# Side work of a gated-MLP kernel's feed-forward and output stages: places from formulas, places from tables

## The chip, the cores and the metric

The kernel runs on one core of one Trainium2 chip. Its time is the device time of one launch in microseconds; a figure is the median of several runs. A core has five engines that each work through a list of their own in order: TensorE (PE in the profile, its weight loads PEld), VectorE (DVE), ScalarE (ACT), GpSimd (POOL) and SyncE (SP). SP only issues DMA transfers here. The engines wait for each other through semaphores.

## The reference

The input x has 2048 tokens of 640 features. With xn = layernorm(x), the kernel computes x + s * silu(B). B is a feed-forward layer, s a linear attention with 32 heads of 20 features and a learned feature map.

```python
B = gelu(xn @ w1 + b1) @ w2 + b2                 # 640 -> 1536 -> 640
q, k, v = heads(xn @ wqkv)
pq, pk = q @ w_phi, k @ w_phi                    # per head, 20 x 20
phi_q = concat(softmax(pq), softmax(-pq))        # 40 features
phi_k = concat(softmax(pk), softmax(-pk))
kv, z = phi_k.T @ v, sum(phi_k)
s = ((phi_q @ kv) / (phi_q @ z + 1e-6)) @ wo
out = x + s * silu(B)
```

## The kernel before

Products of 32-bit numbers are made from three faster products: each operand is split into a high part (one ACT copy that rounds) and a low part (a subtraction on DVE or POOL), and high x high, high x low and low x high are added in PSUM. The large products also use Strassen's scheme with seven block products, which is why sums and differences of blocks (T2, T3, T1, T4 of the activations, S1 to S4 of the weights) are made beside the products.

A first stage, not touched here, projects q, k and v, accumulates kv, and writes the exponentials of the 16 query tiles (128 tokens each, 640 KB) to memory, `e_dram`. The stage after it has an order written out by hand, under `tc.manual_schedule()`, so every engine's list is the order of the program text. It consists of 188 slots:

- slots 0 to 41 (UP0 = 0), first up pass: `up(g)` for the six groups g of hidden features, seven slots each, one block product (`part`) a slot; the results go through gelu into the tiles `hr`;
- slots 42 to 83 (DN0), first down pass, `down(2, ...)`: seven runs of six slots, one for each block product with w2 (A11, A12, S2, S3, S1, S4, A22 in this order), then silu, and the result goes to `g_dram`;
- slots 84 to 125 (UP1) and 126 to 167 (DN1): the same for the other half of the tokens;
- from slot 168 (OUT): the output, four chunks c of 512 tokens with five slots d each: `finish` multiplies the numerators oT with wo, and DVE and POOL multiply with the gate and add x.

A slot first issues its products and what takes them out of PSUM, and then `tick()` runs the side work that is due: functions put into the table `todo` by `when(slot, function)`. Side work is issued at the end of its slot, in the order in which it was entered; `soon(1, ...)` puts work at the head of the next slot, `after(k, ...)` k slots later. An engine executes its list as soon as its waits allow, so a slot is a place in five lists and not a time. The side work is:

- **query tiles** (`plan_q`): `q_load` (SP, from `e_dram`), `q_ez` (POOL, L1536: times the sums of the keys), `q_rc` (DVE, L405 and L1540), `q_dn` (DVE, L1545 to L1552, into a PSUM bank), `q_scale` (POOL, L410), `q_store` (SP, to `phi_dram`). Before, a tile that starts at slot s has them at s-4, s, s+1, s+3, s+4 and s+7;
- **weights of the down products**: `w_load` and `w_make` load and split blocks of w2 (tiles `w2r`, `w2s`); `w_sum` and `w_a35` load the finished sums S1 to S4 that `plan_s` made in slots 2 to 51 (`s_load`, `s_sums`, `s_split`, `s_a35`) and stored to `s_dram`. Before, a block is loaded six slots ahead of its first product, a w2 block split four slots ahead;
- **weights of the second up pass**: in the first up pass `w1_sums`, `w1_step` and `w1_put` make and store them, in the second `w1_raw`, `w1_sum_tiles`, `w1_wa` and `w1_wb` load them and split what is left;
- **forms** (`form`): six slots ahead of a down product, the activation block is split: ACT makes the high part (L1313); for the low part, "bank" has ACT copy the block into a PSUM bank as well (L1312) and DVE subtracts from the bank, "vector" and "pool" subtract straight from SBUF on DVE or POOL (L1317). Before, the first six forms of a pass alternate "pool" and "vector", the other 36 are "bank";
- **reload** and **plan_x**: the operands of the second up pass;
- **numerators**: `load_phi_tile` loads query features, `num_t` transposes them on PE (L1575), `num_m` multiplies with kv (L1586, L1593) and issues small transfers oT<-oTl from ACT's queue. For chunk 0 they lie in the second down pass, for the others in the chunk before.

All loads and stores but oT<-oTl are issued by SP, in one list. `q_store` of a tile and a `store` of a result wait there for the engine that makes it.

## Time and profile before

| | |
|---|---|
| median of 3 runs | 662.82 us (662.77 to 664.23) |
| the profiled execution | 664.42 us |
| its span, first to last instruction | 662.4 us, TensorE clock 1.000 |
| DMA | 154.63 MB, mean 233 GB/s |
| read and written in memory | 98.31 MB, 53.54 MB |

A profile shows one execution. Every instruction has the line of the program that issued it and the names of the tiles that it writes and reads; busy times are sums over instructions, and an idle time is named by what ended it. A product of 128x512 is shown with some 390 ns although the next one starts 230 ns after it, because products overlap in the array. TensorE's idle time is therefore read from the gaps between products, and not from the durations.

### The profile page before, as it was taken

How to read it: one execution, taken by the hardware profiler on the slowest of the kernel's cores; microseconds unless marked ns; L12 is line 12 of the kernel's file. 1: busy time of each engine (PE TensorE's matmuls, PEld its weight loads, DVE VectorE, ACT ScalarE, POOL GpSimd, SP SyncE). 2: the span in 40 equal slices, each digit the busy share in tenths (PEclk: the TensorE clock that was granted, in tenths of full speed). 3: DMA queues.
4: the chain of work that ended last, by engine and by line, in shares of the span. 5: the costliest groups of instructions: out<-in, count | busy, mean ns of one | idle time of the engine just before them, and what ended most of it. 6: DMA issues, size and time to landing. Idle time of an engine off the chain costs nothing. (4 is left out here: it accounts for less than half of the span.)

```text
span 662.4 us, 12226 instructions
## 1 busy us (share of the span) xinstructions
PE 641.4 (97%) x4544; PEld 558.7 (84%) x4544; DVE 453.7 (68%) x718; ACT 387.5 (59%) x693; POOL 439.8 (66%) x382
## 2 busy tenths in 40 slices
PE   9999999999999999999999999998998999999897
PEld 9999999999899998788777888886776787777776
DVE  5878987766875777566896568788998645364142
ACT  4556777644666678556987763223686596513320
POOL 3597887774873467998898756778799620453222
PEclk9999999999999999999999999999999999999999
DMA  8436911032814859885999979773559967989644
GB/s 316 185 120 211 298 62 61 26 97 80 256 81 149 304 206 369 316 299 194 385 319 321 390 268 369 256 276 131 198 206 279 409 227 224 348 294 322 203 147 133
DMA packets 86411, 154.63 MB, mean 233 GB/s; under 512 B 6320, under 2 KB 47792, under 8 KB 85840
## 3 DMA queue, kind: packets, MB, share of 16 engines
q1 hardware_dynamic: 86032, 153.20, 66.0%
q10 hardware_dynamic: 320, 0.66, 0.5%
q8 instruction: 36, 0.59, 0.4%
q14 instruction: 23, 0.19, 0.1%
HBM read 98.31 MB, written 53.54 MB: 229 GB/s over the span
## 5 line engine op out<-in xcount | busy, mean ns | idle before, releaser
L1402 PE MATMUL pB<-hs,w2s 128*128 128x512 f32 x648 | 153.4, 393 | 6.8 <-DMA w2s<-s_dram 1.8
L1402 PEld LDWEIGHTS pB<-hs,w2s 128*128 128x128 f32 x648 | 119.9, 188 | 35.1 <-issue 4.2
L1199 PE MATMUL pB<-xp,w1s 128*128 128x512 f32 x324 | 80.5, 391 | 3.3 <-POOL w1s L1247 1.7
L1199 PE MATMUL pB<-xd,w1s 128*128 128x512 f32 x324 | 79.8, 390 | 0.9 <-POOL w1s L1247 0.9
L1199 PEld LDWEIGHTS pB<-xp,w1s 128*128 128x128 f32 x324 | 60.5, 188 | 17.6 <-DVE pB L1220 2.1
L1648 PE MATMUL pB<-oT,wo 128*128 128x512 f32 (+1 forms) x315 | 71.7, 383 | 2.6 <-DMA oT<-oTl 2.6
L1199 PEld LDWEIGHTS pB<-xd,w1s 128*128 128x128 f32 x324 | 60.7, 188 | 13.9 <-POOL w1s L1247 1.3
L1648 PEld LDWEIGHTS pB<-oT,wo 128*128 128x128 f32 x315 | 56.3, 188 | 15.7 <-issue 2.7
L1254 ACT ACTIVATE hr<-pB,b1t 128x512 f32<-128x512 f32 x48 | 32.6, 686 | 59.1 <-DVE pB L1220 58.8
L1651 POOL TENSOR_TENSOR xres<-gt,xres 128x256 f32<-128x256 f32 x36 | 25.7, 736 | 54.9 <-DVE gt L1650 26.1
L1317 DVE TENSOR_TENSOR hs<-pB,hs 128x512 fp32r<-128x512 f32 x72 | 46.5, 677 | 13.5 <-ACT hs L1313 11.5
L391 POOL TENSOR_TENSOR e<-e,mxs 128x1280 f32<-128x1280 f32 x12 | 28.4, 2371 | 40.4 <-DVE mxs L386 36.0
L1313 ACT ACTIVATE hs<-hr 128x512 fp32r<-128x512 f32 x84 | 52.2, 623 | 2.0 <-PE pB L1402 2.0
L1650 DVE TENSOR_TENSOR gt<-pB,gt 128x256 f32<-128x256 f32 x40 | 15.3, 419 | 54.6 <-PE pB L1648 51.0
L1312 ACT ACTIVATE pB<-hr 128x512 f32<-128x512 f32 x72 | 42.8, 594 | 16.8 <-POOL hr L1299 7.1
L1299 POOL TENSOR_TENSOR hr<-hr 128x512 f32<-128x512 f32 x36 | 49.1, 1388 | 0.0
L397 ACT ACTIVATE e<-e 128x1280 f32<-128x1280 f32 x32 | 40.7, 1273 | 13.5 <-POOL e L391 5.6
L493 PE MATMUL pW<-wsum,xd 128*128 128x320 f32 x288 | 48.4, 310 | 0.0
L410 POOL TENSOR_TENSOR eq<-eq,rc 128x1280 f32<-128x1280 f32 x14 | 33.4, 2385 | 22.0 <-DVE rc L1552 12.1
L493 PEld LDWEIGHTS pW<-wsum,xd 128*128 128x128 f32 x288 | 43.6, 188 | 0.0
L1578 ACT ACTIVATE ph<-pB 120x512 f32<-120x512 f32 (+1 forms) x44 | 23.1, 600 | 33.6 <-PE pB L1575 20.8
L1536 POOL TENSOR_TENSOR ez<-eq,zrep 128x1280 f32<-128x1280 f32 x14 | 42.0, 2998 | 1.1 <-PE pB L1402 1.1
(235 smaller groups left out, 1397.1 us busy)
## 6 DMA issues: line engine op xcount, KB each, us to landing
w2s<-s_dram SPq DMA_DIRECT2D x24, 512.0 KB
e_dram<-e SPq DMA_DIRECT2D x16, 640.0 KB
phi<-phi_dram SPq DMA_DIRECT2D x16, 640.0 KB
eq<-e_dram SPq DMA_DIRECT2D x14, 640.0 KB
phi_dram<-eq SPq DMA_DIRECT2D x14, 640.0 KB
raw<-in_w_dram SPq DMA_DIRECT2D x24, 320.0 KB
w_dram<-w1s SPq DMA_DIRECT2D x12, 512.0 KB
s_dram<-ws SPq DMA_DIRECT2D x12, 512.0 KB
```

The lines of the kernel that those rows point to most:

```text
L397: nc.scalar.activation(ef, ef, AF.Exp)
L410: eng.tensor_tensor(e3, e3, rc[:, :, None].to_broadcast([P, 64, DH]), op=OP.mult)
L493: nc.tensor.matmul(self.bank[ch][:, :HALF], self.x(blk, a), w(b), start=new and i == 0, stop=i == len(mms) - 1, skip_group_check=True)
L1199: nc.tensor.matmul(bank[ch][:], tl[:, a, off + wo_:off + wo_ + P], mov(blk, b), start=new and n == 0, stop=n == len(mms) - 1, skip_group_c ...
L1254: nc.scalar.activation(dst, ps, AF.Gelu_apprx_tanh, bias=b1t[:, f:f + 1])
L1299: nc.gpsimd.tensor_tensor(block(k, g), block(a, g), block(b, g), op=OP.subtract)
L1312: nc.scalar.activation(ps[:], src, AF.Copy)
L1313: nc.scalar.activation(hs[:, 0], src, AF.Copy)
L1317: (nc.gpsimd if lo == "pool" else nc.vector).tensor_tensor(hs[:, 1], ps[:] if lo == "bank" else src, hs[:, 0].bitcast(F32), op=OP.subtract)
L1402: nc.tensor.matmul(ps[:], w(b), hs[:, a, :], start=start and n == 0, stop=stop and n == 2, skip_group_check=True)
L1536: nc.gpsimd.tensor_tensor(qz[t], qe[t], zf[0], op=OP.mult)
L1648: nc.tensor.matmul(ps[:, cols], w, o[:, a, cols], start=n == 0, stop=n == 14)
```

## The change

The formulas that gave the slots of the side work are replaced by a table, `PLAN`, with one number for each piece of work. A number can have a fraction: `when` puts the work into slot `int(s)`, and `tick` sorts a slot's work by the fraction and then by the order of entry; work from `soon` still comes first. The numbers differ from those of the formulas by up to some tens of slots for query tiles (the tiles are also taken in another order: 0, 8, 2, 3, 11, 4, 10, 12, 1, 5, 9, 7, 6, 13, 15, 14) and mostly by less than three slots elsewhere. The low parts of 19 of the 84 forms are made in another way (`lo`). In the output, the phi tiles of a later chunk are loaded at other d (`phi2`). The assertions check that a load from `phi_dram`, `s_dram` or `a35_dram` comes behind its store. No instruction of the products is added or removed.

```diff
@@ -41,6 +41,105 @@
 
 def _ft(t):
     return (120 * t, 120 if t < 10 else 80)
+
+
+PLAN = {
+    "q": [
+        [44, 49, 50, 51, 52, 55],
+        [107.25, 111.25, 114.25, 116.25, 117.25, 120.5],
+        [77, 82, 84, 85.5, 86, 87.5],
+        [79, 83, 87, 89, 102, 107],
+        [89.5, 94, 95, 97, 98, 104.25],
+        [113, 115, 118, 120, 121, 126],
+        [135.25, 139.5, 141.75, 143.0, 147.5, 149],
+        [126.25, 131.25, 131.25, 132.75, 135.25, 138.25],
+        [46.5, 50.5, 51.5, 54.0, 54.5, 57.25],
+        [129, 131, 130.5, 133, 136, 139],
+        [100.75, 102.75, 103.75, 106.75, 108.0, 109.75],
+        [84, 88, 89, 90.5, 92, 93],
+        [105, 109.25, 109, 111, 112, 119],
+        [142.5, 149.5, 147.5, 149.5, 150.5, 154],
+        [168, 170.5, 170, 171, 175, 175.75],
+        [168, 168.75, 169, 170.5, 171, 172],
+    ],
+    "s": [
+        [2.5, 6.0, 8.5, 10.5, 11.5],
+        [7.75, 12.75, 14.75, 18.0, 16.25],
+        [15, 20, 22, 23, 24],
+        [22, 27, 29, 30, 30.5],
+        [26.75, 32, 34.25, 35, 39],
+        [36, 41, 42.5, 43, 44],
+    ],
+    "w": [
+        [36, 38],
+        [40.5, 40.5],
+        [40, 40],
+        [42, 42.25],
+        [44, 44],
+        [44.75, 48],
+        [72, 74],
+        [70, 76],
+        [72, 76],
+        [35, 37],
+        [35.5, 37.5],
+        [40.25, 40.25],
+        [120.5, 123.25],
+        [122, 124],
+        [123.5, 127],
+        [125.5, 127.5],
+        [128, 129.5],
+        [129, 131.5],
+        [156, 158],
+        [158, 159],
+        [160.5, 162],
+        [119.25, 121],
+        [121, 123],
+        [120, 125],
+    ],
+    "ws": [
+        [47.75, 50.75, 51.75, 53.75, 57, 57.5, 66, 68, 70, 59.5, 59.75, 63.75, 60.75, 62.75, 64.75],
+        [132.5, 135.5, 134.5, 137.5, 137.5, 141.5, 149.5, 151.5, 156.0, 143.5, 145.5, 147.5, 144.5, 146.0, 148.5],
+    ],
...
+    "w1_0": [
+        [],
+        [1, 2, 2, 4, 6, 7, 8.25],
+        [7.5, 8.5, 9.5, 10.5, 12.5, 14, 15, 3],
+        [14, 15, 16.25, 17.25, 19, 21, 21, 11],
+        [20, 20, 21, 22, 24, 25, 26, 14],
+        [29, 30, 30.5, 32, 34, 35, 36, 24],
+    ],
+    "phi": [135.75, 135.0, 142.5, 141.5, 166, 163.75, 166.25, 166.25],
+    "num": [152, 152, 154, 156.25, 158.0, 158.5, 156.75, 156, 160, 161.5, 162, 165.25],
...
+    "lo": [
+        ["pool", "vector", "pool", "vector", "pool", "vector", "bank", "bank", "bank", "bank", "vector", "bank", "bank", "bank", "bank", "bank", "bank", "vector", "bank", "vector", "vector", "bank", "bank", "bank", "bank", "bank", "bank", "bank", "bank", "bank", "vector", "bank", "bank", "bank", "bank", "bank", "pool", "pool", "bank", "vector", "bank", "bank"],
+        ["pool", "bank", "pool", "pool", "pool", "vector", "bank", "bank", "bank", "bank", "bank", "bank", "bank", "bank", "bank", "vector", "bank", "bank", "bank", "bank", "bank", "bank", "bank", "bank", "bank", "vector", "bank", "bank", "vector", "pool", "bank", "vector", "bank", "bank", "vector", "bank", "bank", "vector", "pool", "pool", "bank", "bank"],
+    ],
+    "out": [
+        [(6, 0), (5, 0), (0, 11)],
+        [(6, 0), (5, 0), (0, 11)],
+        [(6, 0), (5, 0), (0, 11)],
+    ],
+    "phi2": [
+        [0, 1, 3, 3],
+        [0, 0, 2, 2],
+        [],
+        [],
+    ],
+}
 
 
 @with_exitstack
@@ -1219,20 +1318,20 @@
     def add(out, a, b, eng=nc.vector, op=OP.add):
         eng.tensor_tensor(out, a, b, op=op)
 
-    todo, at_slot = {}, [0]
-
-    def when(s, f, *args):
-        assert s >= at_slot[0]
-        todo.setdefault(s, []).append((f, args))
+    todo, at_slot, seen = {}, [0], set()
+
+    def when(s, f, *args, first=False):
+        assert int(s) >= at_slot[0]
+        todo.setdefault(int(s), []).append((not first, s % 1, len(todo.get(int(s), ())), f, args))
 
     def after(k, f, *args):
         when(at_slot[0] + k, f, *args)
 
     def soon(k, f, *args):
-        todo.setdefault(at_slot[0] + k, []).insert(0, (f, args))
+        when(at_slot[0] + k, f, *args, first=True)
 
     def tick():
-        for f, args in todo.pop(at_slot[0], ()):
+        for *_, f, args in sorted(todo.pop(at_slot[0], ()), key=lambda e: e[:3]):
             f(*args)
         at_slot[0] += 1
 
@@ -1343,26 +1442,22 @@
 
     def w_sum(k, d):
         t = slab(F32R, "w2s", (P, 2, 2, 2 * P))
+        assert {("s", SUMS.index(k) // 2 * 2, g) for g in (2 * d, 2 * d + 1)} <= seen
         load(t[:].bitcast(F32), s_dram[SUMS.index(k)][:, 2 * d:2 * d + 2])
         wt[k, d] = t
 
     def w_a35(d):
+        assert {("a35", 0, g) for g in (2 * d, 2 * d + 1)} <= seen
         load(wt["A5", d][:, :, :, P:].bitcast(F32), a35_dram[:, 2 * d:2 * d + 2])
 
-    def plan_w(s):
-        for i, k in enumerate(("A11", "A12", "S2", "S3", "S1", "S4", "A22")):
+    def plan_w(h):
+        for i, k in enumerate(("A11", "A12", "A22", "A5")):
             for d in range(3):
-                use = s + 6 * i + 2 * d
-                if i == 0:
-                    when(use - 7, w_load, "A5", d)
-                    when(use - 5, w_make, "A5", d, use - 5 > s)
-                if k in SUMS:
-                    when(use - 6, w_sum, k, d)
-                else:
-                    when(use - 6, w_load, k, d)
-                    when(use - 4, w_make, k, d, use - 4 > s)
-        for d in range(3):
-            when(s + 19 + 2 * d, w_a35, d)
+                s, m = PLAN["w"][12 * h + 3 * i + d]
+                when(s, w_load, k, d)
+                when(m, w_make, k, d, m > (DN0, DN1)[h])
+        for i in range(15):
+            when(PLAN["ws"][h][i], w_sum if i < 12 else w_a35, *(((SUMS[i // 3],) if i < 12 else ()) + (i % 3,)))
 
     rws, sts = {}, {}
 
@@ -1382,20 +1477,19 @@
         st = sts[g]
         t = cell((P, 2, 2, 2 * P), F32R, "ws")
         split_late(st[:, k:k + 2], t[:, :, 0, :], t[:, :, 1, :], nc.vector)
+        after(3, seen.add, ("s", k, g))
         store(3, s_dram[k:k + 2, :, g].rearrange("k p b c -> p k b c"), t[:].bitcast(F32))
 
     def s_a35(g):
         src = rws.pop(g)[:, 9]
         t = halves.tile([P, 2, P], F32R, tag="U", name="a35")
         split_late(src, t[:, 0], t[:, 1], nc.vector)
+        after(3, seen.add, ("a35", 0, g))
         store(3, a35_dram[:, g], t[:].bitcast(F32))
 
-    def plan_s(g, s):
-        when(s - 5, s_load, g)
-        when(s, s_sums, g)
-        when(s + 2, s_split, g, 0)
-        when(s + 3, s_a35, g)
-        when(s + 4, s_split, g, 2)
+    def plan_s(g):
+        for s, f, *a in zip(PLAN["s"][g], (s_load, s_sums, s_split, s_a35, s_split), *[(g,) * 5], (None, None, 0, None, 2)):
+            when(s, f, *[b for b in a if b is not None])
 
     def mm3(ps, w, hs, start, stop):
         for n, (a, b) in enumerate(PASSES):
@@ -1411,7 +1505,7 @@
         def step():
             n = at_step[0]
             at_step[0] += 1
-            form(n + AHEAD, los(n + AHEAD))
+            form(n + AHEAD, (los + [None] * AHEAD)[n + AHEAD])
             sum_step()
             tick()
 
@@ -1504,12 +1598,9 @@
         dst = xd()[:, :, :, at(p)]
         split_late(tt[:, a:b], dst[:, a:b, 0, :], dst[:, a:b, 1, :], nc.gpsimd)
 
-    def plan_x(p, s):
-        when(s - 4, xf_load, p)
-        when(s, xf_add, p)
-        when(s + 2, xf_sums, p)
-        when(s + 4, xf_split, p, 0, 4)
-        when(s + 5, xf_split, p, 4, 9)
+    def plan_x(p):
+        for s, f, a in zip(PLAN["x"][p], (xf_load, xf_add, xf_sums, xf_split, xf_split), ((), (), (), (0, 4), (4, 9))):
+            when(s, f, p, *a)
 
     tailp = []
 
@@ -1555,13 +1646,16 @@
         scale_heads(qe[t], qr.pop(t))
 
     def q_store(t):
+        seen.add(t)
         load(phi_dram[t], qe.pop(t))
 
-    def plan_q(t, s, pace=(-4, 0, 1, 3, 4, 7)):
-        for f, k in zip((q_load, q_ez, q_rc, q_dn, q_scale, q_store), pace):
-            when(s + k, f, t)
+    def plan_q(*tiles):
+        for t in tiles:
+            for f, s in zip((q_load, q_ez, q_rc, q_dn, q_scale, q_store), PLAN["q"][t]):
+                when(s, f, t)
 
     def load_phi_tile(c, i, home=None):
+        assert TPC * c + i in seen
         t = (home or slab)(F32R, "phi", (P, 2 * D))
         nc.sync.dma_start(t[:].bitcast(F32), phi_dram[TPC * c + i])
         return t
@@ -1604,6 +1698,7 @@
         for nt, nm in plan:
             now = [(j, p, *num_t(phi, p, j)) for j, p in steps[:nt]]
             del steps[:nt]
+            assert len(turned) >= nm
             for j, p, n, ph in turned[:nm]:
                 num_m(j, oT, p, n, ph)
                 if p and j < 5:
@@ -1682,22 +1777,16 @@
         when(0, q_put, ea[o], 6 + o)
         when((2, 9)[o], q_put, eb[o], 14 + o)
     for g in range(1, NG):
-        s = UP0 + 7 * (g - 1)
-        if g > 1:
-            when(s - 4, w1_next, g)
-        when(s + 1, w1_sums, g)
-        for i, k in enumerate((2, 3, 4, 6)):
-            when(s + k, w1_step, g)
-        for i in range(2):
-            when(s + 7 + i, w1_put, g, i)
+        for s, f, *a in zip(PLAN["w1_0"][g], (w1_sums,) + (w1_step,) * 4 + (w1_put,) * 2 + (w1_next,) * (g > 1), (g,) * 8,
+                            (None,) * 5 + (0, 1, None)):
+            when(s, f, *[b for b in a if b is not None])
     for g in range(NG):
-        plan_s(g, (7, 13, 20, 27, 34, DN0 + 2)[g])
-    LO = lambda n: "bank"
+        plan_s(g)
     for h in range(2):
         s = (DN0, DN1)[h]
         for n in range(AHEAD):
-            when(s - AHEAD + n, form, n, ("pool", "vector")[n % 2])
-        plan_w(s)
+            when(s - AHEAD + n, form, n, PLAN["lo"][h][n])
+        plan_w(h)
     for g in range(NG):
         up(g)
 
@@ -1707,15 +1796,13 @@
         spare.extend(range(4))
 
     when(DN0, start_q)
-    plan_q(0, DN0 + 4)
-    plan_q(1, DN0 + 8)
+    plan_q(*range(16))
     when(DN0 + 16, spare.clear)
     when(DN0 + 17, xds.clear)
-    for i in range(4):
-        when(DN0 + 2 + 4 * i, reload, i)
-        when(DN0 + 18 + 4 * i, reload, 4 + i)
+    for i in range(8):
+        when(PLAN["reload"][i], reload, i)
     for p in range(2):
-        plan_x(p, DN0 + 22 + 7 * p)
+        plan_x(p)
 
     def w1_raw(g):
         w1r_at[g] = load_w1(g, cell)
@@ -1737,24 +1824,17 @@
         w1g_at[g] = w1_dict(w1b.pop(g) + [sl])
 
     for g in range(NG):
-        s = UP1 + 7 * (g - 1)
-        when(s - 3, w1_raw, g)
-        when(s - 1, w1_sum_tiles, g)
-        when(s + 1, w1_wa, g)
-        when(s + 3, w1_wb, g)
+        for s, f in zip(PLAN["w1"][g], (w1_raw, w1_sum_tiles, w1_wa, w1_wb)):
+            when(s, f, g)
     when(UP1 + 9, kv_state, kvr_out[0])
-    for i in range(8):
-        plan_q(2 + i, UP1 - 1 + 5 * i)
-    down(2, LO)
+    down(2, PLAN["lo"][0])
     for g in range(NG):
         up(g)
 
     xstack.close()
     tailp.append(ctx.enter_context(tc.tile_pool(name="late", bufs=8, side="right", reuse_waits="tile")))
     tailp.append(ctx.enter_context(tc.tile_pool(name="phs", bufs=14, side="right", reuse_waits="tile")))
-    for i in range(4):
-        plan_q(10 + i, DN1 + (4, 7, 10, 17)[i])
-    phi, phin, oTs, groups = [], [], {}, {}
+    phi, phin, oTs, groups = {}, {}, {}, {}
 
     def first_oT():
         oTs[0] = new_oT()
@@ -1765,35 +1845,31 @@
         next(groups[0], None)
 
     for i in range(4):
-        when(DN1 + 9 + 3 * i, lambda i=i: phi.append(load_phi_tile(0, i, tall)))
-        when(DN1 + 36 + i, lambda i=i: phin.append(load_phi_tile(1, i)))
+        when(PLAN["phi"][i], lambda i=i: phi.update({i: load_phi_tile(0, i, tall)}))
+        when(PLAN["phi"][4 + i], lambda i=i: phin.update({i: load_phi_tile(1, i)}))
     when(DN1 + 26, first_oT)
-    for n in range(11):
-        when(DN1 + 27 + n, first_num)
-    when(DN1 + 38, first_num)
+    for s in PLAN["num"]:
+        when(s, first_num)
     for j in range(5):
-        when(DN1 + 21 + 2 * j, load_wo)
-        when(DN1 + (26, 28, 30, 32, 38)[j], split_wo)
+        when(PLAN["wo"][j], load_wo)
+        when(PLAN["wo"][5 + j], split_wo)
     for i in range(2):
         when(DN1 + 40 + i, load_res, i)
-    down(0, LO)
+    down(0, PLAN["lo"][1])
 
     oT = oTs[0]
-    for i in range(2):
-        plan_q(14 + i, OUT + 2 + 2 * i, (-2, 0, 0, 1, 2, 3))
     for c in range(NCH):
         nxt, phi2 = iter(()), []
         if c + 1 < NCH:
             oTn = new_oT()
-            nxt = num_groups(phin, oTn, ((6, 0), (5, 0), (0, 11)))
+            nxt = num_groups(phin, oTn, PLAN["out"][c])
         for d in range(KC):
             load_res(c * KC + d + 2)
             finish(c, d, oT, c == NCH - 1 and d >= 3)
             next(nxt, None)
             tick()
-            if c + 2 < NCH and d in (0, 2):
-                for _ in range(2):
-                    phi2.append(load_phi_tile(c + 2, len(phi2)))
+            for _ in range(PLAN["phi2"][c].count(d)):
+                phi2.append(load_phi_tile(c + 2, len(phi2)))
         if c + 1 < NCH:
             oT, phin = oTn, phi2
     while todo:
```

14 lines of the change are left out of this document (added).

## The prediction

> **What bounds the kernel now.** I read the head of the page first: span, then busy time of each engine.
>
> ```profile
> span 662.4 us, 12226 instructions
> PE 641.4 (97%) x4544; PEld 558.7 (84%) x4544; DVE 453.7 (68%) x718; ACT 387.5 (59%) x693; POOL 439.8 (66%) x382
> ```
>
> TensorE is the bound, and the change adds and removes no product. It can only win back time in which TensorE stands still. The busy times by stage say where that is; the columns are the stretch, its length, then busy time and instruction count of PE, PEld, DVE, ACT and POOL, then granted clock, DMA share and GB/s. The stretches are the first up pass, the first down pass, the end of the second up pass, most of the second down pass, the output, and its end.
>
> ```profile
> 239.00:314.00 75.00, 74.12 (x327) 60.89 (x326) 49.03 (x62) 49.49 (x81) 68.53 (x64) 1.00 0.80 288
> 314.00:391.70 77.70, 76.88 (x334) 61.96 (x333) 54.87 (x82) 62.37 (x117) 62.29 (x49) 1.00 0.97 347
> ...
> 430.00:470.00 40.00, 36.73 (x158) 29.05 (x157) 33.99 (x51) 14.24 (x26) 32.25 (x16) 1.00 0.53 188
> 470.00:525.00 55.00, 48.96 (x210) 38.68 (x210) 47.05 (x73) 38.80 (x71) 48.81 (x29) 1.00 0.80 283
> ...
> 560.50:620.00 59.50, 56.86 (x357) 44.57 (x356) 26.80 (x64) 21.60 (x51) 26.67 (x26) 1.00 0.89 301
> ```
>
> Length less PE busy is the idle time: 0.9, 0.8, 3.3, 6.0 and 2.6 us, together 13.65 us. More than two thirds lies in the 95 us around the second entry into the down products. The table of waits, for PE alone, names the causes (us in total, times, longest).
>
> ```profile
> PE pB L1648 <- DMA oT<-oTl: 2.6, 3, 1.0
> PE pB L1199 <- POOL w1s L1247: 2.6, 2, 1.7
> PE pB L1402 <- DMA w2s<-s_dram: 1.8, 2, 1.6
> PE pB L1402 <- issue: 1.6, 1, 1.6
> ...
> PE pB L1402 <- DVE rc L1552: 1.5, 1, 1.5
> PE pB L1402 <- DVE w2s L1247: 1.3, 2, 0.9
> PE pB L1199 <- DVE pB L1220: 1.2, 1, 1.2
> ```
>
> A stop costs more than its gap. In the timeline of PE the 21 products after one of them last 5.04 us, while in the chain that ended last 80 products without a stop take 18.46 us, 0.231 each, or 4.85 for 21. So 0.2 us is lost at each refill.
>
> ```profile
> 506.26 5.04 PE L1402 MATMUL pB<-hs,w2s 128*128 128x512 f32 x21 [1.46 <-DVE rc L1552]
> ```
> ```profile
> 480.92 18.46 PE pB L1402 x80
> ```
>
> Two mechanisms make the large waits. **The first is a loop through POOL and DVE** in the second up pass. Timeline of POOL:
>
> ```profile
> 437.92 2.37 POOL L410 TENSOR_TENSOR eq<-eq,rc 128x1280 f32<-128x1280 f32 x1 [0.30 <-POOL w1s L1247]
> 440.25 2.95 POOL L1536 TENSOR_TENSOR ez<-eq,zrep 128x1280 f32<-128x1280 f32 x1
> 449.74 2.37 POOL L410 TENSOR_TENSOR eq<-eq,rc 128x1280 f32<-128x1280 f32 x1 [6.53 <-issue]
> 452.06 2.92 POOL L1536 TENSOR_TENSOR ez<-eq,zrep 128x1280 f32<-128x1280 f32 x1
> 456.50 1.53 POOL L1247 TENSOR_TENSOR w1s<-raw,w1s 128x640 fp32r<-128x640 f32 x1
> ```
>
> The ez of a tile feeds its q_dn on DVE, that feeds its q_scale on POOL, and the next tile's ez stands behind that scale in POOL's order. One such tile every 5 slots. At 443.2 POOL has nothing it may do, stands 6.53 us, and the low part of the last w1 tile, which PE waits for (1.7), runs only at 456.50. DVE, timeline of the same time, shows why q_dn was late:
>
> ```profile
> 440.42 3.20 DVE L1247 TENSOR_TENSOR w1s<-raw,w1s 128x384 fp32r<-128x384 f32 x1 [1.23 <-ACT w1s L1246]
> 446.69 1.49 DVE L1545 TENSOR_REDUCE pB<-ez 128x64 f32<-128x1280 f32 x1
> 454.79 0.60 DVE L1247 TENSOR_TENSOR w1s<-raw,w1s 128x384 fp32r<-128x384 f32 x1 [1.23 <-ACT w1s L1246]
> ```
>
> The same split takes 0.60 us alone and 3.20 beside an ez: it ended when that ez ended. **The second is SyncE's single order.** Its timeline, and below it its waits from 470 to 525:
>
> ```profile
> 484.44 0.32 SPq L1240 DMA_DIRECT2D w2s<-s_dram  x1
> 497.76 0.32 SPq L1240 DMA_DIRECT2D phi_dram<-eq  x1
> ```
> ```profile
> SPq L1240 <- POOL eq L410: 20.2, 3, 12.9
> ```
> ```profile
> 502.37 10.52 DMA w2s<-s_dram
> ```
>
> The q_store of tile 10 waits 12.9 us for POOL; behind it stand the loads of the S3 sums. The last row (chain) is one of them: issued at 502.37, landed at 512.89, and PE stops there (1.6) and again at 522.6 (1.6).
>
> **The change, part by part.** Slots in us, from the stretches above and the 470 at which the second up pass ends: 78.3/42 = 1.87 in that pass.
>
> *Query tiles.* All 16 keep their six steps, so POOL's 2.4 + 2.95 us and DVE's 4.8 us for each remain. What changes is distance. In the second up pass ez comes at slots 82, 83, 88, 94, 102.75, 109.25, 111.25, 115 instead of 83, 88, ... 118; the scale of tile 3 follows its ez after 19 slots, not 4, so most ez no longer stand behind the scale before. After slot 115 no ez follows, where before one stood at 118: POOL and DVE enter the down products with one tile less behind them. In the second down pass the four ez go from 130, 133, 136, 143 to 131, 131.25, 139.5, 149.5, so POOL has two instead of three in the stretch in which it also makes the sums of hr. Against that, slots 109 to 121 still hold three q_rc and three q_dn (14.4 us of DVE in 24). I take 2.6 of the 3.3 us of 430 to 470; the bounds are 0 and 3.3. Of the waits behind DVE in 470 to 525 (1.5 and 1.3) I take 1.0 and 0.9.
>
> *Block sums (w_sum, SP).* S3.0 and S3.1 go to 137.5, ahead of the stores of tiles 7 and 9 (138.25, 139), and tile 10 is stored in the up pass (109.75). The two waits of 1.6 lose their cause: 3.2, bounds 0 and 3.2. What would be late next is S1 (143.5), behind no store until 149.
>
> *First passes.* The sums of w2 and the splits of w1 go up to two slots earlier: the 0.9 us stop (POOL w1s) should go. Eight forms of the first down pass and eleven of the second take another engine or leave the bank out; net 16 ACT copies into a bank vanish.
>
> ```profile
> L1317 DVE TENSOR_TENSOR hs<-pB,hs x72: 626/679/692, 323.7 to 549.3; 128x512 fp32r<-128x512 f32 x72
> ...
> L1317 DVE TENSOR_TENSOR hs<-hr,hs x6: 677/1229/1783, 311.7 to 477.4; 128x512 fp32r<-128x512 f32 x6
> ```
> ```profile
> L1312 ACT ACTIVATE pB<-hr 128x512 f32<-128x512 f32 x72 | 42.8, 594 | 16.8 <-POOL hr L1299 7.1 <-DVE hs L1317 6.9 <-DVE u L1220 1.9
> ```
>
> ACT saves 16 x 0.594 = 9.5 us and some PSUM banks; DVE pays 12 x (1.229 - 0.679) = 6.6 us, at most 12 x 1.1 = 13. Neither engine is full and the forms stand 6 slots ahead of their product, so nothing of it counts. That cover ends when DVE is more than 6 slots late. For all of this I take 1.0 of the 1.7 us in the two first passes. Four of these lows fall at slots 135, 145, 148 and 151, where DVE has 55 - 47.05 = 8 us to spare; 4 x 0.55 = 2.2 fits. The Trainium skill, "SBUF — State Buffer", section "SBUF: two separate sides", speaks against these lows: a DVE instruction with two SBUF inputs and a GpSimd one that reads SBUF lock each other out for a whole instruction. By that rule, which the 3.20 us row bears out, each could wait out an ez of 2.95, 4 x (2.95 - 0.68) = 9.1 us against 8 to spare, and the sum would be 1.1 us later.
>
> *w_load and w_make.* At slots 40 and 40.5 three pairs of load and split share a slot, before there were two slots between. ACT waits at the split, and the forms and gelu of slot 41 stand behind it. The nearest load (chain):
>
> ```profile
> 472.00 2.93 DMA w2r<-in_w_dram
> ```
>
> Bounds: 0, if SP is early, and 3 x 2.93 = 8.8 us. I take 0.7: the transfers run side by side, and the gelu behind them waited for DVE anyway.
>
> *Output.* Pairs of phi loads move from d = 2 to d = 3 of the first chunk; the last q_scale goes from slot 174 to 175. SP (first fence), ACT's queue (second), chain (third):
>
> ```profile
> 574.82 0.93 SPq L1566 DMA_DIRECT2D phi<-phi_dram  x2
> ...
> 577.76 0.39 SPq L1240 DMA_DIRECT2D out_dram<-xres  x1
> ...
> 600.93 0.32 SPq L1240 DMA_DIRECT2D phi_dram<-eq  x1
> ...
> 601.82 4.10 SPq L1566 DMA_DIRECT2D phi<-phi_dram  x2
> ```
> ```profile
> 579.47 7.34 ACTq L1615 DMA_DIRECT2D oT<-oTl  x5
> ```
> ```profile
> 605.60 6.36 DMA phi<-phi_dram
> ...
> 619.05 1.86 PE pB L1575 x24
> ```
>
> The small oT transfers get stuck behind a phi pair. In the first chunk that pair still goes out just before them (its new place follows the third tile's store, 577.76 before), so that wait stays. In the second chunk the store comes some 4 us later, the phi pair behind it lands near 616 instead of 612, and its transposes, which start at 619.05, would be due at 617.4 without the oT waits of 1.7: those go and a phi wait may come. Bounds of the whole: 2.6 less to 4 more; I take 0. The last num_m one slot later (165) leaves the first oT transfers a slot less: 0.5, bounds 0 and 1.9. The transposes themselves only trade slots.
>
> **Sum.** Gone: 2.6 + 1.9 + 3.2 + 1.0 = 8.7, and ten refills of 0.2 = 2.0. Come: 0.7 + 0.5 + 0.5 for edges that I do not see, a tenth of the 5 us or so that stays. Net 9.0. The profiled run took 664.42 us, 2.0 around its span of 662.4; it becomes 655.4. The median of the runs shown, 662.82, lies 1.6 below the profiled run, so I predict 653.8.
>
> **Rivals.** *A, only the queue gains.* DVE in slots 109 to 121 is as full as before, so the loop's waits return there. Left are 3.2 + 0.4 of refill and 0.4 of the first passes: 4 us, 658.8. For it: the same tiles and instructions; against: the emptier slots 116 to 131. *B, nothing moves.* POOL ran tile 8's ez at 452, some 4 us after its slot 113 (391.7 + 30 x 1.87 = 447.8); an engine that is late does its list back to back wherever the slots are, and the change does not do what it says. 662.8. Against: the 6.53 us hole. *C, ACT stands at its splits.* The pairs of slot 40, and those of 42 and 44, five in all, find SP without lead. If each waits its 2.93 us, ACT loses 14.7 us; one slot of 1.87 is covered by the PSUM banks that stand free, so PE pays up to 12.8, of which 0.7 is counted: 653.8 + 12.1 = 665.9. It decides from the point where a load is issued less than 2.93 us ahead of ACT's turn. For it: first down pass with a DMA share of 0.97. Against: ACT has 77.7 - 62.4 = 15 us to spare there.
>
> **How the numbers follow.** Forecast 0.53, A 0.16, B 0.12, C 0.19. The lower end is everything gone: 13.65 + 15 x 0.2 = 16.6, so 646.2; I take 647. The upper end takes in C and an upper part of the output's bounds: 667. A measurement here tells 0.3%, 2 us, from no change: faster (forecast, nearly all of A) 0.68, same 0.13, slower 0.19.
>
> **What would show it.** Right: PE's waits on w2s from s_dram and on POOL w1s near the second entry into the down products are gone, SP's longest wait on POOL's eq is under 6 us, POOL has no hole over 3 us in the second up pass, and 430 to 525 loses 6 us or more of idle time. Wrong: PE waits in the first down pass behind ACT's split of w2 (C), a phi wait of over 2 us in the output, or holes of POOL and DVE as large as before at other slots (A, B).

## The result, and the profile after

The changed kernel takes 666.83 us (665.41 to 666.92, 4 runs) where the kernel before takes 662.80 in the same comparison: a ratio of 1.0051, interval 1.0032 to 1.0071. It is slower by half a per cent; the prediction said 653.8. The profiled execution took 666.79 us, 1.7 around its span. Line numbers rise by 91 to 99 (the products of the down passes are L1496, the forms L1411, L1412 and L1416, `ez` is L1627).

Head of the page after:

```profile
span 665.1 us, 12237 instructions
...
PE 641.5 (96%) x4544; PEld 561.5 (84%) x4544; DVE 467.5 (70%) x712; ACT 379.3 (57%) x678; POOL 449.0 (68%) x388
```

TensorE does the same 4544 products and is still the bound. The busy times of four of the stretches that the prediction showed (length, then busy time and count of PE, PEld, DVE, ACT, POOL, then granted clock, DMA share, GB/s):

```profile
239.00:314.00 75.00, 72.17 (x311) 58.77 (x310) 50.88 (x62) 47.08 (x77) 66.21 (x63) 0.98 0.84 299
314.00:391.70 77.70, 77.70 (x343) 64.05 (x342) 55.09 (x78) 60.04 (x114) 70.66 (x52) 1.00 0.94 331
...
430.00:470.00 40.00, 40.00 (x178) 33.10 (x178) 33.85 (x54) 17.79 (x31) 36.43 (x19) 1.00 0.59 208
470.00:525.00 55.00, 47.11 (x196) 38.18 (x195) 51.80 (x61) 36.22 (x65) 46.94 (x28) 0.91 0.83 294
```

From 430 to 470 TensorE no longer stands: the 3.3 us of idle time are gone. From 470 to 525 it stands 7.9 us instead of 6.0, and the clock column falls to 0.91: 196 products there, 210 before. The first stretch lost too, 2.8 us of idle time at a clock of 0.98. PE's table of waits says by what (us in total, times, longest):

```profile
PE pB L1496 <- DVE hs L1416: 7.9, 1, 7.9
PE pB L1298 <- POOL w1s L1346: 2.4, 1, 2.4
PE pB L1743 <- DMA oT<-oTl: 2.1, 2, 1.6
PE pB L1298 <- ACT u L1362: 1.9, 1, 1.9
```

In the stages that the change touches, the seven waits quoted of before are replaced by these four over 1 us, and the first alone is larger than any three of the seven. It is one stop, and it ends with one instruction of DVE. Timeline of DVE, then of POOL, around it:

```profile
494.49 1.28 DVE L1416 TENSOR_TENSOR hs<-pB,hs 128x512 fp32r<-128x512 f32 x2
495.69 11.71 DVE L1416 TENSOR_TENSOR hs<-hr,hs 128x512 fp32r<-128x512 f32 x1
507.31 1.87 DVE L1416 TENSOR_TENSOR hs<-pB,hs 128x512 fp32r<-128x512 f32 x3
```
```profile
495.48 1.29 POOL L1398 TENSOR_TENSOR hr<-hr 128x512 f32<-128x512 f32 x1
496.74 2.37 POOL L509 TENSOR_TENSOR eq<-eq,rc 128x1280 f32<-128x1280 f32 x1
499.06 3.73 POOL L1398 TENSOR_TENSOR hr<-hr 128x512 f32<-128x512 f32 x3
502.73 2.89 POOL L1627 TENSOR_TENSOR ez<-eq,zrep 128x1280 f32<-128x1280 f32 x1
505.57 1.27 POOL L1398 TENSOR_TENSOR hr<-hr 128x512 f32<-128x512 f32 x1
507.54 2.53 POOL L1398 TENSOR_TENSOR hr<-hr 128x512 f32<-128x512 f32 x2 [0.69 <-DVE hs L1416]
```

The subtraction is the low part of form 15 of the second down pass, a form that the change made "vector" (`lo`). Beside seven operations of POOL that follow each other without a gap it takes 11.71 us; its neighbours of the same size from the bank take 0.6 to 0.7. It ends at 507.40, 0.56 us after POOL has come to the end of what it may do (505.57 + 1.27); POOL's next operation waits for it. Form 15's product was due at 499.56. The stop of 7.89 us is followed by slow products (timeline of PE):

```profile
507.45 12.90 PE L1496 MATMUL pB<-hs,w2s 128*128 128x512 f32 x44 [7.89 <-DVE hs L1416]
```

44 products in 12.90 us are 0.293 us each, against 0.231. The stop in the first up pass has the same tail. Four windows of 3.41 us, columns as above; the stop is in the second, the clock is 0.50 in the third:

```profile
301.43:304.85 3.42, 3.32 (x15) 2.43 (x13) 1.78 (x3) 1.93 (x4) 3.19 (x5) 1.00 0.70 229
304.85:308.26 3.41, 1.12 (x5) 0.93 (x6) 2.30 (x3) 2.66 (x6) 3.41 (x4) 1.00 0.34 126
308.26:311.67 3.41, 3.41 (x10) 2.67 (x9) 0.69 (x1) 0.03 (x1) 1.36 (x2) 0.50 1.02 282
311.67:315.09 3.42, 3.42 (x17) 2.80 (x16) 2.91 (x5) 2.27 (x4) 0.98 (x1) 1.00 0.88 302
```

That stop (2.39 us, slot 37) is a matter of order on POOL. After, and below it before:

```profile
300.38 1.29 POOL L1346 TENSOR_TENSOR w1s<-st,w1s 128x512 fp32r<-128x512 f32 x1
301.62 4.24 POOL L1474 TENSOR_TENSOR rw<-rw 128x256 f32<-128x256 f32 x5
305.82 1.26 POOL L1346 TENSOR_TENSOR w1s<-st,w1s 128x512 fp32r<-128x512 f32 x1
```
```profile
301.80 2.54 POOL L1247 TENSOR_TENSOR w1s<-st,w1s 128x512 fp32r<-128x512 f32 x2
304.30 4.40 POOL L1379 TENSOR_TENSOR rw<-rw 128x256 f32<-128x256 f32 x5
```

Before, both splits of w1 stand ahead of the five sums of w2; the change moves the sums of the fifth group from slot 34 to 32, and the last split comes 4.2 us late. The stop of 1.9 us in the second up pass (slot 95) is a chain on DVE: a split of w1 that the change moved from slot 87 to 88.5 runs beside an ez and takes 3.06 us in place of 0.60, and two long reductions of query tiles, with the short steps that follow them, stand ahead of the addition (412.41) that the wait hangs on:

```profile
404.62 3.06 DVE L1346 TENSOR_TENSOR w1s<-raw,w1s 128x384 fp32r<-128x384 f32 x1
407.61 1.48 DVE L1636 TENSOR_REDUCE pB<-ez 128x64 f32<-128x1280 f32 x1
...
410.43 1.48 DVE L504 TENSOR_REDUCE rc<-eq 128x64 f32<-128x1280 f32 x1
```

The balance by stage, in us between the first products of slots 0, 42, 84, 126 and 168 and the end, worked out by counting the products in the traces (the other columns belong to the experiments):

| stage | before | after | q_only | no_q | lo2_bank | vec11 | four_edits | out_old |
|---|---|---|---|---|---|---|---|---|
| first up | 74.8 | 78.7 | 73.9 | 74.3 | 76.8 | 78.6 | 74.2 | 74.4 |
| first down | 77.7 | 75.6 | 76.9 | 78.6 | 75.8 | 75.6 | 77.1 | 77.1 |
| second up | 78.4 | 76.6 | 75.4 | 78.0 | 76.6 | 76.6 | 74.3 | 74.3 |
| second down | 90.4 | 95.4 | 88.6 | 90.2 | 84.7 | 84.8 | 86.0 | 83.7 |
| output | 102.0 | 99.5 | 102.7 | 101.3 | 101.2 | 100.2 | 100.4 | 100.4 |

After gains 6.4 us in three stages and loses 8.9 in two. Each column is one profiled execution; that of q_only took 659.04 us, 3 us over the median of its runs.

### The profile page after: what moved, and what is told of

Same layout as the page of the kernel before. It is cut to its first block, busy times and chain, and to the rows that moved or that the text cites. A ratio compares the mean times of both kernels' runs of the same rounds, so it can differ in the third digit from the quotient of the medians.

```text
span 665.1 us, 12237 instructions
## 1 busy us (share of the span) xinstructions
PE 641.5 (96%) x4544; PEld 561.5 (84%) x4544; DVE 467.5 (70%) x712; ACT 379.3 (57%) x678; POOL 449.0 (68%) x388
## 4 chain that ended last, share of the span: by engine, by line
PE 71%; POOL 10%; DVE 8%; DMA 4%; ACT 3%; issue 3%; SPq 0%; POOLq 0%; DVEq 0%; ACTq 0%
PE pW L592 19%; PE pB L1496 18%; PE pB L1298 11%; PE pB L1743 9%; PE pA L451 4%; POOL rw L1474 3%; PE pW L1075 3%; PE pB L1669 2%; DVE hs L1416 2%; PE pA L270 2%; DMA oT<-oTl 2%; PE pB L1680 1%; POOL w1s L1346 1%; POOL st L705 1%; PE kv L684 1%
## 5 line engine op out<-in xcount | busy, mean ns | idle before, releaser
L1496 PE MATMUL pB<-hs,w2s 128*128 128x512 f32 x648 | 153.0, 396 | 7.9 <-DVE hs L1416 7.9
L1496 PEld LDWEIGHTS pB<-hs,w2s 128*128 128x128 f32 x648 | 122.8, 191 | 34.6 <-DVE hs L1416 8.3
L1412 ACT ACTIVATE hs<-hr 128x512 fp32r<-128x512 f32 x84 | 51.3, 623 | 5.2 <-PE pB L1496 5.0
L1627 POOL TENSOR_TENSOR ez<-eq,zrep 128x1280 f32<-128x1280 f32 x14 | 42.3, 3025 | 15.7 <-DMA eq<-e_dram 6.5
L1416 DVE TENSOR_TENSOR hs<-pB,hs 128x512 fp32r<-128x512 f32 x56 | 36.8, 678 | 12.3 <-ACT hs L1412 11.5
L1411 ACT ACTIVATE pB<-hr 128x512 f32<-128x512 f32 x56 | 33.2, 593 | 20.1 <-DVE hs L1416 10.5
```

The costliest lines, as they stand in the source:

```text
L1411: nc.scalar.activation(ps[:], src, AF.Copy)
L1412: nc.scalar.activation(hs[:, 0], src, AF.Copy)
L1416: (nc.gpsimd if lo == "pool" else nc.vector).tensor_tensor(hs[:, 1], ps[:] if lo == "bank" else src, hs[:, 0].bitcast(F32), op=OP.subtract)
L1496: nc.tensor.matmul(ps[:], w(b), hs[:, a, :], start=start and n == 0, stop=stop and n == 2, skip_group_check=True)
L1627: nc.gpsimd.tensor_tensor(qz[t], qe[t], zf[0], op=OP.mult)
```

## The experiments

**Is it the one subtraction?** Form 15's low part is given back to the bank or to POOL in the changed kernel, and put alone into the kernel before. Edits of the table are written here as single entries.

```diff
-PLAN["lo"][1][15] = "vector"
+PLAN["lo"][1][15] = "bank"          # lo15_bank; "pool" in lo15_pool
```
```diff
-    down(0, LO)
+    down(0, lambda n: "vector" if n == 15 else "bank")     # before_vec15, in the kernel before
```

> The changed kernel with one entry put back: the low part of form 15 of the second down pass (slot 135) reads from a PSUM bank instead of SBUF. Theory P (port): that subtraction took 11.71 us because POOL ran from 495.48 to 506.84 without a gap and a DVE instruction with two SBUF inputs is not let in before POOL has a gap; TensorE stood 7.89 us for it and then ran 13 products at half clock (2.6 us). So 7.9 + 2.6 = 10.5 us go, 666.8 becomes 656 to 657.5, and the first stop in that pass is under 2 us. Theory D (DVE is late there in any case, for the two query tiles reduced just before): the bank form waits nearly as long, at most 3 us go, 664 or more.

> As lo15_bank, but the low part of form 15 goes to POOL, where it stands in POOL's own order and no ACT copy comes back. Theory P: it no longer has to win a port, so the same 10.5 us go, less the 1.3 us that POOL gets more: 656 to 659. Theory D: as little as with the bank, 664 or more. A third theory, that the ACT copy into a bank matters (a bank held back ACT), would have this one lose less than 5 us while lo15_bank loses 10.

> The kernel before with nothing changed but the low part of form 15 of the second down pass, which reads from SBUF. Theory P: POOL ran without a gap from 475 to 519 there, so the subtraction, due near 494, gets in only where POOL itself has to wait for a q_dn that stands behind it on DVE, near 504: 8 to 11 us for it, and TensorE, whose products need it at 501 to 503, stands 2 to 6 us: 665 to 670. Theory D: the subtraction takes what such ones took in the kernel before, 1.8 us at most, and the time stays within 1 us of 662.8.

lo15_bank: 659.32 us, ratio 0.9959 [0.9937, 0.998] to the kernel before. One word of the table is worth 7.5 us, and without it the change is faster. lo15_pool: 661.62, 0.998 [0.9964, 0.9996]. Both are above what was expected, by 1.8 and 2.6 us, and the trace of lo15_bank shows a cause: the next "vector" form of the pass, 25, is now the long one, as it is in lo15_pool with 7.95 us (DVE, then POOL, of lo15_bank):

```profile
509.19 7.96 DVE L1416 TENSOR_TENSOR hs<-hr,hs 128x512 fp32r<-128x512 f32 x1
```
```profile
510.05 2.40 POOL L509 TENSOR_TENSOR eq<-eq,rc 128x1280 f32<-128x1280 f32 x1
512.38 2.98 POOL L1627 TENSOR_TENSOR ez<-eq,zrep 128x1280 f32<-128x1280 f32 x1
515.28 1.32 POOL L1416 TENSOR_TENSOR hs<-hr,hs 128x512 fp32r<-128x512 f32 x1
```

In the kernel before, the same word makes the same kind of row:

```profile
494.08 8.89 DVE L1317 TENSOR_TENSOR hs<-hr,hs 128x512 fp32r<-128x512 f32 x1
```

But before_vec15 takes 663.06, 1.0013 [0.9987, 1.0039]: no difference that can be told in the median, a miss against the 665 to 670 expected. Its ten times form two groups, six from 661.3 to 663.8 us and four from 665.5 to 667.6, where 30 of the 31 executions of the kernel before stay under 665.1; the profiled one, 665.48, is of the upper group. New stops of 3.76 and 1.09 us stand in its trace, and the old stops at 512.93 and 522.56 (1.6 each) are gone; it seems that what would have waited there was in time once PE was late. The mechanism is not a thing of the new tables. What it costs differs between executions, and no run shows why.

**The sums of slot 32.**

```diff
-        [26.75, 32, 34.25, 35, 39],
+        [26.75, 34, 34.25, 35, 39],      # PLAN["s"][4], sums34
```

> The changed kernel with one entry put back: the five subtractions that make the w2 sums of group 4 go from slot 32 to slot 34, behind the last split of w1 instead of ahead of it. Theory O (order on POOL): the 2.39 us stop of TensorE at 307.1 is these 4.2 us of subtractions standing ahead of the split, and the eight products at half clock behind it cost 1.6 more; both go: 666.8 becomes 662.5 to 663. Theory F (POOL is full in that pass, 66 of 75 us busy, and late with everything): less than 1 us goes.

664.51 us, 1.0028 [1.0012, 1.0045]: 2.3 us less than after, where about 4 were expected. The stop of 2.39 us is gone, and one of 1.37 stands at the end of slot 42. There ACT waits at a split of w2 for its load, and the gelu that PE waits for stands behind that split:

```profile
317.15 0.63 ACT L1345 ACTIVATE w2s<-w2r 128x512 fp32r<-128x512 f32 x1 [1.37 <-DMA w2r<-in_w_dram]
...
318.41 0.67 PE L1272 MATMUL pB<-kvr,ident 128*128 128x240 f32 x2 [1.37 <-ACT hr L1353]
```

The same stop stands in four_edits (1.18 us), out_old (1.17) and no_q (1.40), where the five sums have their old place and the loads and splits of w2 the new ones (ACT waits 0.72 to 0.96 there), and in neither before nor q_only, where the loads and splits of w2 have the old ones. So the five sums do not make it; by the rows it is what rival C described, at one place instead of five. In the changed kernel ACT waits 1.23 us there, and PE, already late from the stop at slot 37, does not wait. No run moves the table of w2 (`w`) alone, so this cause is argued.

**All low parts of the pass, the numerators, and the four misplaced pieces together.**

```diff
-PLAN["lo"][1][n] = "vector"   # n = 15, 25, 28, 31, 34, 37
+PLAN["lo"][1][n] = "bank"     # lo2_bank
-PLAN["num"][-1] = 165.25
+PLAN["num"][-1] = 164.25      # lo2_num: this too
-PLAN["s"][4] = [26.75, 32, 34.25, 35, 39]
+PLAN["s"][4] = [29, 34, 36, 37, 38]
-PLAN["w1"][1][3] = 88.5
+PLAN["w1"][1][3] = 87         # four_edits: these two as well
```

> The changed kernel with all six "vector" low parts of the second down pass (forms 15, 25, 28, 31, 34, 37) made by the bank again. Theory P (a DVE subtraction from two SBUF tiles stands still as long as POOL works without a pause): with form 15 alone undone, form 25's subtraction took 7.96 us and left stops of 1.16 and 0.69 us; both should go: 656 to 657.5 us against 659.3. Theory C (DVE is crowded in this pass, the subtractions only show it): the vector lows save DVE nothing and the bank costs ACT six copies of 0.6 us, so the stops stay and the time is within 1 us of 659.3, or above it.

> The same, and the last num_m of the output stage one slot earlier (164.25 in place of 165.25). If the stop at the start of the output stage (1.60 us after, 2.15 us and a half clock behind it with form 15 alone undone) is the transposed tile that this multiplication feeds: 2 to 3 us less than the run with the six low parts alone, about 654. If the transfers stand behind the loads of SP's queue anyway: no difference, within 0.5 us.

> The same two edits, and the last group of partial sums at the places of before (29, 34, 36, 37, 38 in place of 26.75, 32, 34.25, 35, 39), and the last w1 split of the second up pass at 87 in place of 88.5. If the stop of 2.39 us in slot 37 with its 3.41 us of half clock belongs to the order of the sums and the split on POOL, and the stop of 1.85 us in slot 95 to the w1 split on DVE beside the query tile's multiplication: 3.5 to 4 and 1.9 us less, 648 to 650, faster than both kernels. If the stop in slot 37 only moves to slot 42 as it did with the sums at 34: 651 to 652.

lo2_bank: 656.68 us, 0.9915 [0.9884, 0.9945], as expected of P. lo2_num: 657.25, 0.9917 [0.9884, 0.995]: no gain, so the numerator's slot is not what makes the stop at slot 168 (1.82 us in this trace). four_edits: 652.37, 0.9842 [0.9813, 0.9871]; the stops at slots 37 and 95 are gone. The stop at slot 42 (1.18) is there, the case for which 651 to 652 was expected, and the one at slot 168 (2.08) remains.

**Whose gain is it?** q_only has the places of before in every table but that of the query tiles, and the old low parts. no_q is the kernel of the four edits with the query tiles at the old places.

> The changed kernel with the places of before in every table but that of the query tiles, and the low parts as before (all by the bank). If the loop through POOL, DVE and POOL in the second up pass gave what the prediction gave it (2.6 us there, 1.9 behind it) and SP's order needs the loads' table as well: 657 to 659. If the places of the query tiles clear SP's queue too (the stores of the query tiles are what the loads waited behind): 654 to 656. If what was gained came from the loads and splits: within 1 us of 662.8.

> The kernel of the four edits, with the query tiles at the places of before: the counterpart of the run with the query tiles alone. If the gains are the query tiles' (656.0 with them alone, of 662.7): 658 to 661. If they are shared between the tables: about 656. If the other tables only pay with the query tiles moved: 662 or more.

q_only: 655.99 us, 0.9896 [0.9868, 0.9925]. no_q: 662.20, 0.9984 [0.9959, 1.001]. The query tiles bring 6.7 of the 10.3 us of the four edits; the other tables bring nothing that can be told by themselves, and about 3.6 with the query tiles moved (656.0 to 652.4). That the loads of the sums come free of SP's queue is also the query tiles' doing: PE's waits for w2s from s_dram are gone in q_only, whose loads stand where they stood.

**The stop at slot 168.** In out_old, the tables of phi loads, num_m and wo of the four edits go back to the places of before.

> The kernel of the four edits, with the places of before in the tables of phi loads, num_m and wo. In the run of the four edits the output stage begins with a stop of 2.08 us for the transposed tile, whose transfers stand behind four phi loads of 640 KB; before had no stop there. If those tables make it: 650 to 651 against 652.4. If the stop stays: within 0.5 us of 652.4.

649.98 us, 0.9797 [0.9765, 0.9829]: the fastest version, 2.0% below the kernel before. SP's phi loads, the five oT transfers on ACT's queue and PE's first output product, in four_edits and below it in out_old:

```profile
537.92 0.82 SPq L1660 DMA_DIRECT2D phi<-phi_dram  x2
...
540.44 1.25 SPq L1660 DMA_DIRECT2D phi<-phi_dram  x2
...
543.74 3.83 ACTq L1710 DMA_DIRECT2D oT<-oTl  x5
...
550.05 3.68 PE L1743 MATMUL pB<-oT,wo 128*128 128x512 f32 x15 [2.08 <-DMA oT<-oTl]
```
```profile
536.26 1.91 SPq L1597 DMA_DIRECT2D phi<-phi_dram  x3
...
543.63 3.83 ACTq L1647 DMA_DIRECT2D oT<-oTl  x5
...
547.69 3.56 PE L1680 MATMUL pB<-oT,wo 128*128 128x512 f32 x15
```

With the phi loads issued some 2 to 4 us earlier, the small transfers behind them are there in time. phi, num_m and wo were not tried apart, so that the phi loads are the cause is argued from these rows and not shown. From 430 to 525 PE's table of waits now has a single row, 0.5 us.

**Why does that subtraction lose, when others do not?** In 13 traces of the kernel and its variants some 570 operations of two SBUF inputs on DVE started while POOL was in an operation that another followed within 60 ns (POOL's memsets left out). All but five waited for the end of that operation at most (once, in q_only, for the one after it, where the two had started together). The five are form 15 and form 25. In the trials everything of the kernel is left out. ScalarE opens each trial; POOL then has a run without a wait in it, and DVE comes to a subtraction of two SBUF inputs after m subtractions from a bank:

```python
for k, w in enumerate(RUNS[r]):
    nc.gpsimd.tensor_tensor(room[k % 6][:, :w], g[:, :w].bitcast(F32), raw[3][:, :w], op=OP.add)
for k in range(m):
    nc.vector.tensor_tensor(out[k % 6][:], bank[:], (out[(k - 1) % 6] if k else g)[:, :512].bitcast(F32), op=OP.subtract)
h = out[(m - 1) % 6] if m else g
nc.vector.tensor_tensor(low[n % 2][:], raw[0][:, :512], h[:, :512].bitcast(F32), op=OP.subtract)
```

> Everything of the kernel is left out; in its place stand 30 trials, each begun by ScalarE when the one before has ended. In a trial POOL does a run of 4 to 18 operations of two SBUF inputs (128x512 or 128x1280) without a wait between them, and DVE does 0 to 21 subtractions from a bank (one PSUM input) and then one of two SBUF inputs (low<-raw,out), which so falls at different places of the run. Theory P (DVE's subtraction stands still until POOL pauses): in every trial it lasts to the end of POOL's run, up to 13 us in the runs of 18. Theory H (it waits for one POOL operation, as 45 of the 48 such subtractions in four traces do, and the three long ones have another cause): in every trial at most the rest of one POOL operation and 0.7 us, 2.0 us among operations of 128x512 and 3.7 among those of 128x1280. If some trials go one way and some the other: the place in the run decides, and the table of trials shows by what. The subtractions from the bank should take 0.6 to 0.7 us in all cases.

None of the 30 subtractions waited for more than one operation of POOL; the longest took 3.4 us. Theory P, as it stood, falls: a run without a gap is not enough. The five long ones had another thing in common: POOL had been at work for 15 us or more since it last paused or let DVE in. Two runs put that to the test, one in the kernel and one with longer runs by themselves.

```diff
-PLAN["lo"][1][11] = "bank"
+PLAN["lo"][1][11] = "vector"         # vec11, all else as in the changed kernel
```

> The changed kernel with one more "vector" low part: form 11 of the second down pass, due four slots before form 15's. In the traces so far a subtraction of two SBUF tiles on DVE gets in behind one POOL operation wherever the last one did so less than 15 us before (wins after up to 14.9 us), and is kept out for as long as POOL has work where POOL has been at work undisturbed for 15.1 us or more (15.1, 18.4, 18.4, 33.7, 34.9 us: the five long ones). Theory S (it is that stretch that decides): form 11's comes about 11 us after the last one, gets in, and so form 15's comes 7 us after it and takes at most 3.6 us in place of 11.7; the stop of 7.9 us goes and the time is 658 to 661, though one subtraction more stands on DVE. Theory L (the place or the tiles of form 15 decide, or chance): its 11.7 us and the stop stay, 666 to 668.

> The whole computation is left out again: 21 trials, now with runs of 44 POOL operations of 128x512 (F), 20 of 128x1280 (G), or 40 mixed (H), each 53 to 75 us without a wait, and DVE's subtraction of two SBUF tiles after 6 to 45 subtractions from the bank, so 4 to 33 us into the run. Theory S (a stretch of 15 us of POOL undisturbed shuts DVE out): the trials up to about 15 us take at most 3.6 us, those with 21 or more before them (15.2 us in) last to the end of POOL's run, 20 to 55 us. If all 21 stay under 3.6 us: the stretch alone does not do it, and something of the kernel that these trials lack (other engines at work, waits met on the way) has to come with it.

vec11: 656.20 us, 0.9908 [0.9885, 0.993], below the 658 to 661 expected. One more subtraction of the suspected kind makes the kernel 10.6 us faster. Form 11's low part and form 15's, on DVE:

```profile
485.90 2.27 DVE L1416 TENSOR_TENSOR hs<-hr,hs 128x512 fp32r<-128x512 f32 x1
496.13 1.09 DVE L1416 TENSOR_TENSOR hs<-hr,hs 128x512 fp32r<-128x512 f32 x1
```

The first lets POOL's run be broken after 10 us, and the second, at the place that cost 11.71 us, takes 1.09; form 25's, 7.96 in lo15_bank, takes 1.50. So neither the place nor the tiles make it long. lock_long, DVE's rows of two trials, both in runs of 44 operations of 128x512, the second later in its run:

```profile
91.21 1.03 DVE L73 TENSOR_TENSOR low1x<-raw0x,out5x 128x512 fp32r<-128x512 f32 x1
```
```profile
148.92 39.08 DVE L73 TENSOR_TENSOR low0x<-raw0x,out2x 128x512 fp32r<-128x512 f32 x1
```

The table of those that lie near the edge, from the traces of both trials (start in us after the run began, operations that POOL had finished by then, duration):

```
run             start  finished  took
44 of 512       13.0   10         1.03
44 of 512       15.2   12        39.08   to the end of the run
20 of 1280      23.9    8         2.31
20 of 1280      32.6   11        24.81   to the end of the run
40 mixed        19.5   10         1.00
40 mixed        23.9   12        51.40   to the end of the run
18 of 512       14.5   11         0.82
18 of 512       15.2   12         1.31
```

So a long undisturbed run of POOL is enough by itself, and 15 us, the edge that was expected, is not it: 23.9 us in, a subtraction still got in. By the number of operations it is cleaner. After up to 8 undisturbed ones DVE always got in, in the kernel and in the trials; from 14 on it never did; between 9 and 12 both happened (in the kernel it lost after 9 and 12; after 12 operations of 128x512 it lost in a run of 44 and got in in a run of 18). What sets the edge, and why a lost subtraction then loses every handover, stays open.

## Why the prediction was wrong

**The step that failed** is the low parts: "Neither engine is full and the forms stand 6 slots ahead of their product, so nothing of it counts." The instructions were priced rightly in all cases but one, and that one decides: form 15's took 11.71 us where at most one ez, 2.95, was allowed for it. The cover failed as well. It was named (six slots, 11.2 us) and not looked up: the subtraction started at 495.69 for a product due at 499.56, 3.9 us or two slots ahead, because DVE was already late: from 481.7 on it never paused for more than 0.21 us. 11.71 less 3.87 is 7.84, the stop of 7.89 us. The sentence beside it drew on the Trainium skill, "SBUF — State Buffer", section "SBUF: two separate sides", by which a DVE instruction with two SBUF inputs and a GpSimd one that reads SBUF shut each other out for one whole instruction, and the loser waits for the first to finish. All but five of the 570 or so operations agree, if the one in q_only is counted in; the five long ones do not, and neither do eight of the trials.

**Refills** were priced at 0.2 us a stop. That holds for stops up to 1.8 us; after the long ones the clock halves: a window of 3.41 us at half clock has 10 products, the next one 17 (rows above), about 1.4 us lost. After the stop of 7.9 us the halved clock held through three windows, the first of them lying within the stop.

**First passes**: 1.0 us was to be won, 3.9 were lost in the first up pass and 2.1 won in the first down pass. With the five sums back at slot 34 (sums34) the two passes take 74.5 and 77.3 us, together 0.7 less than before and 2.5 less than after, so the loss is the order of the sums and the w1 split on POOL. That order could have been read from the diff and the timeline of before; the prediction does not use it. The stop of 0.9 us that was to go is not in the traces of q_only and before_vec15 either, whose first up pass has the old order: it seems to belong to the one execution.

**w1 split at 88.5**: not in the list of steps at all, 1.85 us. The prediction does not add up DVE's load in slots 88 to 97.

**The last num_m** was priced at 0.5, bounds 0 and 1.9; the stop of slot 168 came (1.6), and its cause was another: with num_m at its old slot it stayed (1.82 in lo2_num). It went with the tables of phi, num_m and wo together, and the rows point to the phi loads of the next chunk ahead of the oT transfers, which the step "output" looked at only in later chunks.

**w_load and w_make** were put at 0.7. Nothing of it shows in the changed kernel; where the stop of slot 37 is gone, a stop of 1.2 to 1.4 us stands at slot 42.

**What was right, and what only in part.** The loop: the 3.3 us of idle time from 430 to 470 went, 2.6 taken. But the second up pass as a whole won 1.8, since 2.2 us of idle time came from 391.7 to 430, where before had none, and POOL's hole moved instead of going. The prediction's sign was no hole over 3 us in that pass; POOL stands 8.77 us, longer than the 6.53 of before, again for a q_dn on DVE:

```profile
416.04 2.37 POOL L509 TENSOR_TENSOR eq<-eq,rc 128x1280 f32<-128x1280 f32 x1 [8.77 <-DVE rc L1643]
```

That is a part of the sign that the prediction gave for rivals A and B. The hole alone costs nothing: in four_edits one of 6.13 us stands at the same place, PE does not stop behind it, and the pass takes 74.3 us. From 430 to 525 the idle time fell from 9.3 to 7.9 us, where 6 or more were to go, because of form 15. The queue: the waits for w2s from s_dram are gone, and SP's longest wait for eq from 470 to 525 is 2.5 us, not 12.9:

```profile
SPq L1339 <- POOL eq L509: 3.6, 2, 2.5
```

The sum for both and the waits behind DVE, 7.7 and its refills, is somewhat more than what q_only measures, 6.7. The moved loads were not needed for it. The output was put at 0 and gained 2.5, inside its bounds. Rival C came with 1.2 to 1.4 us instead of 12.1, and not in the changed kernel, whose first down pass has no wait of PE in it. None of the rivals was what made the kernel slower; the one on the slower side named ACT, and it was DVE.

## What to carry to other kernels

A cover counted in slots is worth the distance at which the instruction really starts, so read that from a timeline before a cost is called hidden. Where POOL gets a longer list without pauses, the price of a two-SBUF operation on DVE can jump from one operation of POOL to all that POOL has left; keep such operations on DVE either frequent enough to break the list or out of it. When a table moves hundreds of pieces of work, look at the order of each engine's list around every piece that moved: here a group of sums, a split of w1, the tables of phi, num_m and wo, and the low parts of one pass hid a gain of 2%.

## What the runs showed of the hardware that was not expected

**DVE can be shut out for good while POOL works.** Up to 8 undisturbed operations, DVE's subtraction goes next; after 14 or more it waits for POOL's pause, 51.4 us in one trial. Subtractions with one input in PSUM took 0.63 to 0.69 us throughout.

**The clock is granted by windows of 3.413 us, and the edge is a little over half a window.** In all traces in which it changes, the changes lie whole multiples of 3.413 us apart. Of the windows at full clock, every one in which PE stood 1.92 us or more was followed by one at 0.50, and none with 1.80 or less. Between the two both came: 1.81 (q_only, from 581.93 us) and 1.82 (lo2_num) halved the clock, 1.85 (lo15_pool) did not. Two windows of lo2_num and one of lo15_pool with their successors (length less PE busy is 1.80, 1.82 and 1.85):

```profile
301.55:304.97 3.42, 1.62 (x8) 1.00 (x6) 2.70 (x4) 2.09 (x5) 3.26 (x5) 1.00 0.74 231
304.97:308.38 3.41, 2.82 (x12) 2.36 (x13) 1.37 (x2) 1.73 (x4) 3.08 (x3) 1.00 0.65 194
550.73:554.14 3.41, 1.59 (x8) 1.02 (x7) 1.23 (x2) 1.40 (x2) 0.00 (x0) 1.00 0.70 221
554.14:557.55 3.41, 3.41 (x10) 2.66 (x9) 0.00 (x0) 0.00 (x0) 0.00 (x0) 0.50 0.82 200
```
```profile
410.39:413.80 3.41, 1.56 (x9) 0.96 (x7) 3.38 (x4) 1.27 (x3) 0.00 (x0) 1.00 0.77 306
413.80:417.21 3.41, 3.41 (x15) 2.83 (x16) 3.13 (x10) 0.53 (x1) 1.76 (x1) 1.00 0.00 0
```

A stop of 2.39 us that lies across the border of two windows costs no clock (lo2_num, 0.59 of it in the second), and the same stop inside one does (after). A part of the 2 to 4 us by which executions of one kernel differ goes with the clock: of the executions of the kernel before that were timed beside lo15_bank, the 11 with a granted clock of 0.997 took 663.4 us in the mean, the 11 with 1.000 took 662.5. The Trainium skill, "TensorE: Matmul & The Clock Gate", section "Part 1: The HAM clock gate", has the free-running windows of 3413 ns, and puts the drop behind an idle window; the rows show that 53% of a window can be enough.
